# A table for the first nine tiles of a fused attention and MLP kernel, with earlier loads of two tiles and casts one tile further ahead

**The chip, the cores and the metric.** The kernel runs on one core of one Trainium2 chip. The metric is device time in microseconds (us), median of several executions; lower is better. An execution is called slow when it lies over 1.5% above the fastest of the same kernel. The ratios leave them out, the quoted medians and ranges do not; all profiles are of fast executions. The results are correct to the reference's tolerance unless a run is said to be wrong.

## The reference

A decayed linear attention (a state per head, multiplied by a factor per token) is followed by a dense layer with a SoLU activation, a layer norm and a second dense layer. Cut to what matters:

```python
B, H, S, D = 4, 8, 768, 64;  d_ff = 1024
for t in range(S):
    state = gamma * state + outer(k[:, :, t], v[:, :, t])
    y[:, :, t] = q[:, :, t] @ state / sqrt(D)
x = y, heads side by side            # [3072, 512]
h = x @ w_in                         # [3072, 1024]
u = h * softmax(h)
ln = (u - mean(u)) / sqrt(var(u) + 1e-6) * g_ln
out = ln @ w_out                     # [3072, 512]
```

The kernel works in chunks ("tiles") of 128 tokens: 4 batches of 6 tiles, 24 in all. Inside a tile the attention is matmuls; between tiles of a batch a state is carried on.

## The kernel before

One list of operations is written in Python. Each names its engine and what it reads and writes; the waits between engines are worked out from the list. So the place of an operation in the list sets its place in its engine's queue, and nothing else. For each tile `t`:

- loads of k, q, v by DMA; casts to bf16 (`ck`, `cq`, `cv`; the last also multiplies by the decay), mostly on Pool;
- transposes of k and q on TensorE into the PSUM bank `Tp`, evacuated to `qkT`;
- `scores` (TensorE into `PT`), `mask` (DVE), `inter` and `intra` (TensorE into `Yp`), `state` (TensorE into `Sp`) with its evacuation `st`, and `y` (DVE, makes `xT`);
- `mm1` (xT times w_in, into two halves of `Hp`), `expo` on ACT, `umul` on DVE (makes u), `square` on ACT and five tiny statistics on Pool;
- transposes of u into the same bank `Tp`, evacuated to `uT`; `mm2` (uT times the second weight, into `Zp`); `z_out`, which scales and stores.

The weights need work first: w_in is cast, w_out is multiplied by g (`w_g_cast`), its column mean is formed on TensorE, and `centre` subtracts it on DVE. Two first tiles use the uncentred weight and a correction, so that they need not wait for the centring.

The opening of the kernel before is written out by hand, and then a loop follows (cuts marked):

```python
loads(0)
load_w_in()
loads(1)
load_g()
load_w_out()
for t in range(2, NRAW):           # NRAW = 6
    loads(t)
setup_consts()
warm(5)                            # matmuls of zeros, they keep TensorE's clock up
cast_qk(0, "dve")
# ... cut: tile 0, tile 1, casts of the weights
for kt in range(KT2):
    colmean(kt)
colmean_out()
square(1)
cast_qk(2, "dve")
# ... cut
mm2(0)
z_out(0)                           # correction on DVE, then scaling on ACT, then the store
t_qk(2)                            # transposes, then qkT on ACT
for kt in range(3):
    centre(kt)
inter(2)
mm2(1)
scores(2)
mask(2)
z_out(1)
cast_qk(3)
cast_v(3)
t_qk(3)
for kt in range(3, 6):
    centre(kt)
intra(2)
state(2)
y_evac(2)
# ... cut: mm1 of tile 2 follows only here

for j in range(3, NT + 2):
    on(loads, j + 3)
    on(intra, j)
    on(state, j)
    on(scores, j + 1)
    on(casts, j + 2)
    # ... cut: t_qk(j+2), umul(j-1), y, st, square, stats, mask(j+1)
    on(mm2, j - 2)
    on(z_out, j - 2)
    # ... cut: t_u and u_evac of j-1, mm1 and expo of j, inter(j+1)
```

The softmax here doesn't subtract the row's maximum and nothing guards it: scores larger than these inputs give would overflow.

## Time and profile before

| | kernel before |
|---|---|
| time, median of the first 3 runs | 168.51 us (167.45 to 168.52) |
| span of the profiled run | 166.9 us |
| TensorE busy | 147.4 us, 88% |
| DVE, ACT, Pool busy | 72%, 64%, 57% |
| mean granted TensorE clock | 0.949 of full |
| mm1 of tile 2 starts at | 40.04 us |

The view gives, for each stretch of the span, the busy us of each engine with the number of instructions, the granted clock, the busy share of the 16 DMA engines and GB/s. Of the kernel before:

```profile
core 0: us, PE busy (x) PEld busy (x) DVE busy (x) ACT busy (x) POOL busy (x), PEclk, DMA share, GB/s
...
20.00:26.00 6.00, 5.13 (x17) 2.08 (x19) 4.87 (x11) 1.99 (x5) 4.38 (x6) 0.64 1.05 226
26.00:40.00 14.00, 8.46 (x76) 4.47 (x74) 10.62 (x16) 4.90 (x7) 10.59 (x15) 0.81 0.91 187
40.00:46.00 6.00, 5.74 (x46) 3.13 (x47) 5.10 (x10) 2.85 (x6) 0.52 (x2) 0.60 1.10 218
46.00:52.00 6.00, 4.93 (x62) 3.24 (x65) 4.15 (x8) 3.41 (x8) 3.79 (x8) 1.00 0.20 46
```

TensorE is busy for only 8.46 of 14 us in the second stretch, and in the first and third it is busy at little more than half speed. ACT is busy for 4.90 of 14: it mostly stands and waits. Note also the last line: DMA moves 46 GB/s there, although most of the tiles are still to be loaded.

### The profile page before, as it was taken

How to read it: one execution, taken by the hardware profiler on the slowest of the kernel's cores; microseconds unless marked ns; L12 is line 12 of the kernel's file. 1: busy time of each engine (PE TensorE's matmuls, PEld its weight loads, DVE VectorE, ACT ScalarE, POOL GpSimd, SP SyncE). 2: the span in 40 equal slices, each digit the busy share in tenths (PEclk: the TensorE clock that was granted, in tenths of full speed). 3: DMA queues.
4: the chain of work that ended last, by engine and by line, in shares of the span. 5: the costliest groups of instructions: out<-in, count | busy, mean ns of one | idle time of the engine just before them, and what ended most of it. 6: DMA issues, size and time to landing. Idle time of an engine off the chain costs nothing. (4 is left out here: it accounts for less than half of the span.)

```text
span 166.9 us, 3716 instructions
## 1 busy us (share of the span) xinstructions
PE 147.4 (88%) x1403; PEld 84.6 (51%) x1427; DVE 120.7 (72%) x231; ACT 106.4 (64%) x204; POOL 95.7 (57%) x197
## 2 busy tenths in 40 slices
PE   1995699565979999999999999999999999999962
PEld 0442434232546555666556555656565656555530
DVE  5275778859778767977787678877887789778540
ACT  7856334303657758776867587767775777667651
POOL 3201787980172885678557855696568656833430
PEclk9999559785699999999999999999999999999999
DMA  5999999976920877987899689896997699111102
GB/s 119 322 346 241 364 209 224 221 160 166 211 67 2 208 179 177 198 209 181 181 189 230 157 190 185 206 211 156 201 237 194 155 192 223 68 67 63 58 26 105
DMA packets 81058, 29.61 MB, mean 177 GB/s; under 512 B 76432, under 2 KB 76432, under 8 KB 81040
## 3 DMA queue, kind: packets, MB, share of 16 engines
q1 hardware_dynamic: 81040, 29.37, 75.2%
q8 instruction: 11, 0.18, 0.5%
q14 instruction: 7, 0.06, 0.1%
HBM read 23.07 MB, written 6.29 MB: 176 GB/s over the span
## 5 line engine op out<-in xcount | busy, mean ns | idle before, releaser
L412 PE MATMUL Hp<-w_in,xT 128*128 128x512 bf16 x188 | 47.9, 399 | 1.4 <-DVE xT L406 1.3
L471 PE MATMUL Zp<-w,uT 128*128 128x512 bf16 x157 | 37.5, 379 | 2.5 <-ACT out_sb L489 1.4
L339 ACT ACTIVATE qkT<-Tp 128x1024 bf16<-128x1024 bf16 x24 | 24.5, 1022 | 18.6 <-PE Tp L335 18.6
L354 DVE TENSOR_TENSOR ptm<-PT,tri 128x1024 bf16<-128x1024 f32 x24 | 29.2, 1216 | 6.5 <-PE PT L347 6.5
L412 PEld LDWEIGHTS Hp<-w_in,xT 128*128 128x128 bf16 x192 | 18.4, 101 | 20.2 <-issue 3.3
L471 PEld LDWEIGHTS Zp<-w,uT 128*128 128x128 bf16 x176 | 16.2, 98 | 17.5 <-DVE uT L465 1.5
L447 POOL TENSOR_SCALAR chain<-sq,chain 128x1 f32<-128x1 f32 x24 | 6.4, 266 | 30.8 <-ACT sq_junk L434 30.6
L419 ACT ACTIVATE e_1<-Hp 128x512 bf16<-128x512 f32 x24 | 14.3, 597 | 11.9 <-PE Hp L412 11.9
L419 ACT ACTIVATE e_0<-Hp 128x512 bf16<-128x512 f32 x24 | 14.3, 597 | 10.5 <-PE Hp L412 10.5
L465 DVE COPY uT<-Tp 128x1024 bf16<-128x1024 bf16 x24 | 16.4, 684 | 2.3 <-PE Tp L459 2.1
L406 DVE TENSOR_TENSOR xT<-Yp,ytab 128x512 bf16<-128x512 f32 x24 | 16.5, 686 | 0.2
L489 ACT ACTIVATE out_sb<-Zp,rstd 128x512 f32<-128x512 f32 x22 | 14.9, 679 | 2.1 <-PE Zp L471 2.1
L425 DVE CUSTOM_DVE_ANT_0 u_1<-Hp,e_1 128x512 bf16<-128x512 f32 x12 | 8.3, 691 | 9.3 <-ACT e_1 L419 9.3
L453 POOL TENSOR_TENSOR rstd<-chain,mhalf 128x1 f32<-128x1 f32 x24 | 13.2, 550 | 2.0
L425 DVE CUSTOM_DVE_ANT_0 u_0<-Hp,e_0 128x512 bf16<-128x512 f32 x12 | 8.3, 690 | 7.9 <-ACT e_0 L419 7.9
L434 ACT ACTIVATE sq_junk<-u_1 128x1024 bf16<-128x1024 bf16 x12 | 12.6, 1050 | 1.9 <-DVE su L425 1.9
L434 ACT ACTIVATE sq_junk<-u_0 128x1024 bf16<-128x1024 bf16 x12 | 12.6, 1050 | 0.9 <-DVE su L425 0.9
L441 POOL TENSOR_SCALAR chain<-se 128x1 f32<-128x1 f32 x24 | 6.5, 269 | 11.3 <-ACT e_0 L419 8.6
L425 DVE CUSTOM_DVE_ANT_0 u_1<-Hp,e_1,su 128x512 bf16<-128x512 f32 x12 | 9.0, 751 | 4.9 <-ACT e_1 L419 4.9
L347 PE MATMUL PT<-qkT 64*128 64x128 bf16 x192 | 9.8, 222 | 2.3 <-ACT qkT L339 2.2
L425 DVE CUSTOM_DVE_ANT_0 u_0<-Hp,e_0,su 128x512 bf16<-128x512 f32 x12 | 9.0, 751 | 3.6 <-ACT e_0 L419 3.6
L323 POOL TENSOR_TENSOR v_1<-v_raw,vtab 128x512 bf16<-128x512 f32 x6 | 6.3, 1043 | 8.4 <-DMA v_raw<-in_v_dram 8.3
(94 smaller groups left out, 251.8 us busy)
## 6 DMA issues: line engine op xcount, KB each, us to landing
k_raw<-in_k_dram SPq DMA_DIRECT2D x24, 256.0 KB, 3.7
q_raw<-in_q_dram SPq DMA_DIRECT2D x24, 256.0 KB, 4.3
v_raw<-in_v_dram SPq DMA_DIRECT2D x24, 256.0 KB, 4.6
out_dram<-out_sb SPq DMA_DIRECT2D x24, 256.0 KB, 2.2
w_in_st<-in_moe_w_in_dram SPq DMA_DIRECT2D x4, 512.0 KB, 5.7
w_out_st<-in_moe_w_out_dram SPq DMA_DIRECT2D x4, 512.0 KB, 5.3
g_sb<-in_moe_g_ln_dram SPq DMA_DIRECT2D x1, 4.0 KB, 4.4
```

The costliest lines, as they stand in the source:

```text
L339: op("act", lambda e: e.activation(out=qkT[sT][:], in_=Tp[:], func=ACT.Copy), w=[("qkT", sT)], ps=[("T", "r")])
L347: op("pe", lambda e, p=p, h2=h2, rows=rows: e.matmul(PT[:, 4 * h2 + p, :], qkT[sT][rows, 4 + p, :], qkT[sT][rows, p, :], start=True, stop= ...
L354: op("dve", lambda e: e.tensor_tensor(out=ptm[s][:], in0=PT[:], in1=tri[:].unsqueeze(1).to_broadcast([128, 8, 128]), op=ALU.mult), r=["tri ...
L406: op("dve", lambda e: e.tensor_tensor(out=xT[s][:], in0=Yp[:], in1=ytab[:, c, :, :], op=ALU.mult), r=[("ytab", p) for p in range(NPAIR)], ...
L412: op("pe", lambda e, kt=kt: e.matmul(Hp[:, hf, :], xT[s][:, kt, :], w_in16[:, kt, 512 * hf:512 * hf + 512], start=(kt == 0), stop=(kt == K ...
L419: op("act", lambda e: e.activation(out=e16[s][:, 512 * hf:512 * hf + 512], in_=Hp[:, hf, :], func=ACT.Exp, accum_out=se[ss][:, hf:hf + 1]) ...
L425: op("dve", lambda e: e.tensor_tensor_reduce(out=u16[s][:, 512 * hf:512 * hf + 512], in0=Hp[:, hf, :], in1=e16[s][:, 512 * hf:512 * hf + 512],
L434: op("act", lambda e: e.activation(out=sq_junk[:], in_=u16[s][:], func=ACT.Square, accum_out=sq[ss][:]), r=[("u16", s, 0), ("u16", s, 1)], ...
L453: op("pool", lambda e: e.tensor_tensor(out=rstd[ss][:], in0=ch[:, 3:4], in1=mhalf[:], op=ALU.pow), r=[("ch3", sc), "mhalf"], w=[("rstd", ss)])
L465: op("dve", lambda e: e.tensor_copy(out=uT[s][:], in_=Tp[:]), w=[("uT", s)], ps=[("T", "r")])
L471: op("pe", lambda e, kt=kt, w=w: e.matmul(Zp[:, :], uT[s][:, kt, :], w[:, kt, :], start=(kt == 0), stop=(kt == KT2 - 1)), r=[("uT", s), (w ...
L489: op("act", lambda e: e.activation(out=out_sb[so][:], in_=Zp[:], func=ACT.Copy, scale=rstd[ss][:, 0:1]), r=[("rstd", ss)], w=[("out_sb", s ...
```

## The change

Its intent is to keep TensorE fed from the start. The hand-written opening goes, and a table gives the order of all operations of the first nine tiles (and the regular part up to tile 12), and for some of them the engine. A local search made the table. Loads of tile 1 now come ahead of w_in and those of tile 2 (with k and q of tile 3) ahead of w_out; w_out's casts are on DVE and ACT, none on Pool any more; casts run up to three tiles ahead instead of two; there are eight raw buffers for each of q, k and v instead of six, and four sets of statistics instead of three. A store may stand apart from its output scaling. The core of the diff, cut:

```diff
+PROLOGUE = """
+Lk.0 ck.0 Lv.1 cv.1 Lq.0 cq.0:dve warm.6 clr.0 Lv.0 Lk.1 t_k.0 warm.6 t_q.0 qkT.0:dve warm.3 scores.0 cv.0
+state.0 Lq.1 Lwi.3 wi0.3:act mask.0 wi1.3:act ck.1 cq.1 Lwi.1 Lwi.2 wi1.1:act t_k.1 intra.0 wi0.1:act Lwi.0 st.0
+Lq.2 cq.2 t_q.1 Lk.2 qkT.1:dve wi1.2:act Lv.2 wi0.2:act Lq.3 y.0 ck.2 cv.2 state.1 Lk.3 Lwo.2 wi0.0:act warm.2
+scores.1 inter.1 mask.1 wi1.0:act Lg.0 Lwo.0 cq.3 warm.11 mm1_0.0 e0.0 Lwo.1 intra.1 mm1_1.0 ck.3 st.1:act Lwo.3
+Lv.3 y.1 u0.0 t_k.2 t_q.2 e1.0 qkT.2:dve Lk.4 u1.0 mm1_0.1 statsA.0 e0.1 state.2 inter.2 Lq.4 Lv.4 sq.0 stats.0
+scores.2 mm1_1.1 Lk.5 t_k.3 st.2 t_q.3 mask.2 u0.1 intra.2 y.2 Lq.5 Lv.5 Lk.6 qkT.3 warm.2 t_u0.0 Lq.6 e1.1
+inter.3 wg.4:dve Lv.6 wg.1:act wg.3:dve wg.5:dve Lk.7 t_u1.0 wg.6:dve wg.0:act scores.3 mask.3 wg.2:act wg.7:act
+mm1_0.2 warm.7 colmean.0 cv.3 state.3 intra.3 e0.2 u0.2 Lq.7 u1.1 Lv.7 Lk.8 Lq.8 Lv.8 Lk.9 uT.0:act Lq.9 Lv.9
+ck.4 cq.4 y.3 cm_out.0 ctr.4 ctr.1 t_k.4 ctr.5 ctr.7 mm1_1.2 ck.5 sq.1 t_q.4 qkT.4 e1.2 u1.2 mm2.0 st.3:act cq.5
... (some 20 more lines of the table are cut)
+"""
-    NRAW, N16, NQT, NOUT = 6, 4, 4, 4
+    NRAW, N16, NQT, NOUT = 8, 4, 4, 4
-        NST = 3
+        NST = 4
+        def evac(eng, out, in_, **deps):
+            if eng == "act":
+                op(eng, lambda e: e.activation(out=out, in_=in_, func=ACT.Copy), **deps)
+            else:
+                op(eng, lambda e: e.tensor_copy(out=out, in_=in_), **deps)
... (the stages take an engine now; their instructions are the same)
+        default = {"ck": "pool", "cq": "pool", "qkT": "act", "st": "dve", "uT": "dve", "z": "act"}
+        for item in PROLOGUE.split():
+            item, _, eng = item.partition(":")
+            name, t = item.rsplit(".", 1)
+            if name == "warm":
+                warm(int(t), None)
+            else:
+                put(name, int(t), eng or None)
+        for j in range(0, NT + 2):
+            for n in ("Lk", "Lq", "Lv"):
+                put(n, j + 5)
... (intra, state, scores, as before)
+            for n in ("ck", "cq", "t_k", "t_q", "qkT", "cv"):
+                put(n, j + 2)
+            for n in ("ck", "cq", "cv"):
+                put(n, j + 3)
... (the rest of the loop, as before; put() leaves out what the table has done)
```

In the table `L` is a load, `wi0.3` the cast of one half of w_in's slice 3, `wg` a cast of w_out, `ctr` a centring, `t_k` and `t_q` are input transposes, `t_u` transposes of u, `e` the exponential, `u` the product, `sq` the square, `clr` a matmul that clears the state. `:act` or `:dve` names the engine where it is not the default.

## The prediction

> **What bounds the kernel now.** I read first the page's 40 slices, then the time line of TensorE for the first matmul group (mm1, into Hp) of each tile, then single waits in the opening. In the slices a column is 4.17 us and a digit tenths.
>
> ```profile
> PE   1995699565979999999999999999999999999962
> PEclk9999559785699999999999999999999999999999
> DMA  5999999976920877987899689896997699111102
> ```
>
> TensorE is full from about the 12th slice; its holes lie before 50 us. So do all the slices with a low granted clock. DMA is full for the first eight slices and has a hole in slices 11 to 13. Next, mm1 of tiles 0, 1, 2, 4, 5, 6 and 23 on TensorE (start, duration):
>
> ```profile
> 12.12 1.67 PE L412 MATMUL Hp<-w_in,xT 128*128 128x512 bf16 x7
> ...
> 20.87 3.19 PE L412 MATMUL Hp<-w_in,xT 128*128 128x512 bf16 x7 [0.98 <-DVE xT L406]
> ...
> 40.04 3.59 PE L412 MATMUL Hp<-w_in,xT 128*128 128x512 bf16 x8 [0.31 <-DVE xT L406]
> ...
> 53.44 1.89 PE L412 MATMUL Hp<-w_in,xT 128*128 128x512 bf16 x8
> ...
> 58.79 1.89 PE L412 MATMUL Hp<-w_in,xT 128*128 128x512 bf16 x8
> ...
> 64.48 1.89 PE L412 MATMUL Hp<-w_in,xT 128*128 128x512 bf16 x8
> ...
> 156.59 1.67 PE L412 MATMUL Hp<-w_in,xT 128*128 128x512 bf16 x7
> ```
>
> From tile 4 to tile 23 the pitch is (156.59 - 53.44) / 19 = 5.43 us. The loop is TensorE's own work; the view by stretches gives TensorE 93.00 busy us of the 94 between 63 and 157. But the first four tiles took 53.44 us: 19 us between mm1 of tiles 1 and 2 alone. A steady pitch would have put tile 4 at 12.12 + 4 x 5.43 = 33.8. The opening is the loss. Two lines of TensorE's time line, and under them two of ACT's, show how it is lost:
>
> ```profile
> 35.22 0.62 PE L335 MATMUL Tp<-ident,qk_3 128*128 128x128 bf16 x8
> ...
> 39.12 0.61 PE L347 MATMUL PT<-qkT 64*128 64x128 bf16 x8 [1.97 <-ACT qkT L339]
> ```
>
> ```profile
> 37.43 0.72 ACT L485 ACTIVATE out_sb<-z_tmp,rstd 128x512 f32<-128x512 f32 x1 [6.33 <-DVE z_tmp L482]
> 38.06 1.01 ACT L339 ACTIVATE qkT<-Tp 128x1024 bf16<-128x1024 bf16 x1
> ```
>
> The transposes of tile 3 ended at 35.8. Their evacuation stood in ACT's queue behind an output that waited 6.33 us for DVE, which was busy centring w_out. TensorE idled 1.97 us, and its clock was lowered after such holes (granted 0.64 in 20 to 26 us, 0.60 in 40 to 46).
>
> **What the Trainium skill says.** (1) "TensorE: Matmul & The Clock Gate", Part 1, architectural detail: ACT and DVE are strict FIFO. The ACT lines above agree. That is why a mere reordering can pay. (2) The same page, "The HAM clock gate": an idle window of about 3.4 us halves the clock, a busy one restores it. The trace agrees in kind: eight mm1 matmuls take 3.59 us at 40.04 and 1.89 at 53.44. (3) "DMA: Bandwidth & Descriptors", Specifications: transfers under 512 B do not reach line rate. Agreed: q, k and v come in 256 B runs (76432 of 81058 packets are under 512 B), and one 256 KB load is consumed about every 1.15 us at the start (casts at 4.22, 5.38, 6.53), 228 GB/s. Two w_in slices of 512 KB came 1.4 us apart (casts at 10.50 and 11.90), 374 GB/s. (4) "GPSIMD Engine Reference", Specifications: Pool shares SBUF interfaces with VectorE. Agreed: a DVE cast that ran beside Pool took 1.268 us, its like alone 0.427.
>
> **The change, part by part.**
>
> *Loads.* The first loads become k0, v1, q0, v0, k1, q1, then w_in, then q2, k2, v2, q3, k3, then w_out. The first four tensors are not needed alone: mm1 of tile 0 now waits for 1.57 MB of tiles plus 2.1 MB of w_in instead of 0.79 + 2.1. At the spacings above: k0 at 4.2, then five loads at 1.15 give q1 at 10.0, then four slices at 1.3 to 1.4 give the last of w_in at about 15.3. ACT has two half casts left (about 0.6 each), so mm1 of tile 0 starts near 16.4: **4.3 us later** than now. In return tile 1 is ready with it. Before this, TensorE transposes and scores tiles 0 and 1, filled up with warming matmuls.
>
> *Work from 16.4 us to the end of mm1 of tile 4.* The table has, on TensorE, with the start-to-start pitches of 58 to 64 us: five mm1 at 1.73 (8.7), five input transposes at 0.67 (3.3), four scores at 0.33 (1.3), four inter at 0.32 (1.3), five intra at 0.30 (1.5), four state and a clear (1.3), three transposes of u at 0.45 (1.35), two mm2 at 1.52 (3.0), the column mean (8 x 0.22 = 1.7) and nine warming matmuls (1.9): **25.4 us**. DVE has: masks 3.4 at 1.14, y 4 x 0.60, u 4 x 1.50, two copies at 0.6, four w_out casts at 0.65, four centrings at 0.69 and one mean correction 0.8, about **19 us**. ACT, counted in the same way (eight exponentials 5.5, two squares 2.3, three qkT and three uT 5.7, four w_out casts 2.6, the rest 3), has **19 us**. The table moves st, uT and two output scalings between DVE and ACT to balance them. TensorE is the heaviest.
>
> *The waits in it.* I walked the table by hand through the five queues with these durations. TensorE is nearly always fed, since two tiles' fronts are ready before the first u. The places that wait: around 23.5 us for Tp (one bank serves qkT and uT), and 25 to 27 us for the last w_out slices, for which DVE's and ACT's casts stand in the queue ahead of mask(3) and e(2). There the table has seven warming matmuls. The walk ends mm1 of tile 4 at 43.4, that is 27.0 us for 25.4 of work. No walk of mine has all semaphore delays, slowed casts and clock dips, so I allow 1.6 us more: 45.0. Today it ends at 53.44 + 1.73 = 55.2.
>
> *What is then still owed.* At that point the new order has done one mm2 and one u transpose less (1.52 + 0.45), and inter, intra and a cleared state more (about 1.2): 0.8 us behind. Gain: 55.2 - 45.0 - 0.8 = **9.4 us**.
>
> *Afterwards.* Tiles 4 to 8 are TensorE-bound today already, so their order can only keep the gain; my walk of tiles 5 and 6 gave 5.4 us a tile. The loop after tile 12 is the old one, except that casts run three tiles ahead. TensorE waits there for no cast now, so that is worth nothing by itself. NRAW 8 and NST 4 only allow the table's reach. The tail (157 to 167, TensorE busy 5.33 of 10) is unchanged. 168.5 - 9.4 = 159.1; I say 159.5.
>
> **Rivals.**
>
> *A: loads bind the opening.* 16.4 depends on six 256 B-run loads at 1.15 us. In 26 to 40 us DMA moved only 187 GB/s, 1.4 us a load. Loads as slow as that would put the first mm1 at 17.7 and, by w_out, the column mean 2 to 3 us later. For it: DMA is full in the first eight slices. Against: the casts at 4.22 to 6.53 show the faster rate just there. It would make 162 to 164.
>
> *B: in-order queues jam.* A table tuned to modelled durations can place an operation ahead of one that is ready, as z did above, at 25 to 27 us most likely, or uT and squares on ACT from 39 to 46 us, where ACT's list is dense. Stores stand in SP's queue behind loads up to tile 11, so store(0) could leave late and hold the fourth output buffer; I expect it out around 48 us and needed around 57. Each hole also risks half clock for a window of 3.4 us (1.7 us). Two such: 162 to 163.
>
> *C: the walk is right and the clock never falls.* 157 to 158.
>
> *D: nothing gained,* if the later start (4.3 us) and 14 more warming matmuls (37 against 23) eat it. By 55.2 us today's order has done about 28 us of TensorE work, counted with the same pitches (five mm1, three mm2, the column mean, seven input transposes, six scores, four u transposes, the rest 4.3), so 27 are lost. The new order has about 3.3 us of useful work behind it at 16.4, so 13 lost; no view shows what would eat the other 14. Unlikely.
>
> **Range and chances.** C bounds it below at about 156.5; A or B alone gives up to 163.5. Slower than 165.2 (2%) would need A and B together and more. Faster 0.93, same 0.05, slower 0.02.
>
> **What would show it.** mm1 of tile 0 near 16.4 (right for loads, 17.7 for rival A); mm1 of tile 1 within 5 us of it; mm1 of tile 2 between 24 and 27 instead of 40.04; mm1 of tile 4 ending at 43 to 47; mm1 pitch afterwards still 5.43; the PEclk row without 5s after the fifth slice; TensorE busy us about unchanged or lower with a shorter span. I am wrong if the loop's pitch changes (casts one tile further ahead would then matter, or a store holding z), or if a single wait of more than 3 us appears on TensorE between 16 and 45 us.

## The result, and the profile after

| | before | after |
|---|---|---|
| time, median of 4 runs each | 167.98 us (167.18 to 168.52) | 161.38 us (161.09 to 161.62) |
| span of the profiled run | 166.9 us | 159.9 us |
| TensorE busy | 147.4 us | 146.6 us |
| DVE / ACT busy | 120.7 / 106.4 us | 113.9 / 110.9 us |
| mean granted clock | 0.949 | 1.000 |

The ratio is 0.961, with a 95% interval from 0.9557 to 0.9663. (Ratios are the mean time of one kernel's fast runs over that of the other's of the same rounds, so they are not quite the ratios of the medians quoted.) The change is faster by 3.9%, 6.6 us by the medians, 7.0 us by the two profiled spans.

The slices of the page, 4.0 us each, after:

```profile
PE   1979979689997999999999999999999999999961
PEclk9999999999999999999999999999999999999999
DMA  5999989999989999998991099999888310111112
```

The holes in TensorE's row are gone but for a few tenths, the clock row has no 5 any more, and DMA stays full until about 84 us, where it pauses, instead of pausing at 46 to 54. Then mm1 on TensorE. In the opening the table issues its two halves apart, four matmuls each. The lines are, in order, the first half of tile 0, the second of tile 1, the first and second of tile 2, the second of tile 4, the first of tile 5, and the whole of tiles 6, 10 and 23:

```profile
16.30 1.04 PE L451 MATMUL Hp<-w_in,xT 128*128 128x512 bf16 x4
...
21.97 1.04 PE L451 MATMUL Hp<-w_in,xT 128*128 128x512 bf16 x4
...
25.68 1.04 PE L451 MATMUL Hp<-w_in,xT 128*128 128x512 bf16 x4
...
32.61 1.03 PE L451 MATMUL Hp<-w_in,xT 128*128 128x512 bf16 x4
...
44.90 1.04 PE L451 MATMUL Hp<-w_in,xT 128*128 128x512 bf16 x4
...
49.93 1.03 PE L451 MATMUL Hp<-w_in,xT 128*128 128x512 bf16 x4
...
55.50 1.89 PE L451 MATMUL Hp<-w_in,xT 128*128 128x512 bf16 x8
...
79.33 1.89 PE L451 MATMUL Hp<-w_in,xT 128*128 128x512 bf16 x8
...
149.33 1.89 PE L451 MATMUL Hp<-w_in,xT 128*128 128x512 bf16 x8
```

Tile 0 starts 4.2 us later than before, and tile 2's first half 14.4 us earlier. Tile 4's mm1 ends at 45.8 (its successor starts 0.87 us after its second half's start) against 55.2. By tile 10, where both kernels have come to the same order, the gain is 86.38 - 79.33 = 7.05 us, and it stays: from tile 10 to tile 23 the pitch is (149.33 - 79.33) / 13 = 5.38 us, before it was (156.59 - 86.38) / 13 = 5.40. (The line of the kernel before at 156.59 has seven matmuls of eight; with the missing record about 0.2 us earlier, the two pitches are the same.) From tile 6 to tile 10 the new kernel takes longer, 23.8 us against 21.9: there it makes up an mm2 and a u transpose that it had put off. TensorE's busy time hardly moved. What went is idle time and time at half clock before 55 us.

What still waits after the change? TensorE's two longest idle stretches between 12 and 100 us:

```profile
31.58 0.32 PE L435 MATMUL Sp<-v_3,qk_3 128*64 128x64 bf16 x8 [1.18 <-POOL v_3 L361]
...
49.70 0.40 PE L375 MATMUL Tp<-ident,qk_3 128*128 128x128 bf16 x4 [0.93 <-POOL qk_3 L349]
```

Behind both stands Pool (buffer 3 is tile 3 in the first, tile 7 in the second). Pool's time line:

```profile
30.48 1.04 POOL L361 TENSOR_TENSOR v_3<-v_raw,vtab 128x512 bf16<-128x512 f32 x1 [6.09 <-DMA v_raw<-in_v_dram]
...
47.47 0.61 POOL L349 CAST qk_3<-k_raw 128x512 bf16<-128x512 f32 x1
48.05 1.04 POOL L361 TENSOR_TENSOR v_3<-v_raw,vtab 128x512 bf16<-128x512 f32 x1
49.03 0.61 POOL L349 CAST qk_3<-q_raw 128x512 bf16<-128x512 f32 x1
```

The first waited 6.09 us for its load. The others waited for nothing: Pool was simply behind with its own list. And DVE, in the stretch where it might have worked ahead, stood for a load of w_out:

```profile
27.77 0.88 DVE L312 TENSOR_SCALAR w_g<-w_out_st,g_sb 128x512 bf16<-128x512 f32 x2 [2.84 <-DMA w_out_st<-in_moe_w_out_dram]
```

### The profile page after: what moved, and what is told of

Its sections match the earlier page's. It is cut to its first block, busy times and chain, and to the rows that moved or that the text cites. A ratio compares the mean times of both kernels' runs of the same rounds, so it can differ in the third digit from the quotient of the medians.

```text
span 159.9 us, 3767 instructions
## 1 busy us (share of the span) xinstructions
PE 146.6 (92%) x1441; PEld 82.3 (51%) x1441; DVE 113.9 (71%) x222; ACT 110.9 (69%) x215; POOL 94.9 (59%) x198
## 5 line engine op out<-in xcount | busy, mean ns | idle before, releaser
L451 PE MATMUL Hp<-w_in,xT 128*128 128x512 bf16 x192 | 46.8, 380 | 0.0
L513 PE MATMUL Zp<-w,uT 128*128 128x512 bf16 x176 | 41.6, 379 | 1.4 <-ACT out_sb L310 1.4
L368 ACT ACTIVATE qkT<-Tp 128x1024 bf16<-128x1024 bf16 x19 | 19.4, 1023 | 14.8 <-PE Tp L375 14.7
L451 PEld LDWEIGHTS Hp<-w_in,xT 128*128 128x128 bf16 x192 | 17.1, 98 | 16.6 <-ACT w_in L310 0.5
L310 ACT ACTIVATE out_sb<-Zp,rstd 128x512 f32<-128x512 f32 x19 | 12.9, 679 | 3.5 <-PE Zp L513 2.8
L370 DVE COPY uT<-Tp 128x1024 bf16<-128x1024 bf16 x17 | 11.7, 686 | 4.0 <-PE Tp L502 3.9
L340 PE MATMUL Zp<-ones_bf,zeros_bf 128*128 128x512 bf16 x37 | 10.8, 431 | 3.5 <-DVE zeros_bf L299 3.5
L480 POOL TENSOR_SCALAR chain<-se 128x1 f32<-128x1 f32 x24 | 7.0, 292 | 6.8 <-ACT e_0 L458 4.5
L483 POOL TENSOR_SCALAR chain<-su 128x1 f32<-128x1 f32 x24 | 6.9, 288 | 5.3 <-DVE su L464 3.9
```

The lines of the kernel that those rows point to most:

```text
L310: op(eng, lambda e: e.activation(out=out, in_=in_, func=ACT.Copy, scale=scale), **deps)
L340: op("pe", lambda e: e.matmul(Zp[:], zeros_bf[:], ones_bf[:].unsqueeze(1).to_broadcast([128, 4, 128]), start=True, stop=True), r=["zeros_b ...
L368: op(eng, lambda e: e.activation(out=out, in_=in_, func=ACT.Copy), **deps)
L370: op(eng, lambda e: e.tensor_copy(out=out, in_=in_), **deps)
L451: op("pe", lambda e, kt=kt: e.matmul(Hp[:, hf, :], xT[s][:, kt, :], w_in16[:, kt, 512 * hf:512 * hf + 512], start=(kt == 0), stop=(kt == K ...
L513: op("pe", lambda e, kt=kt, w=w: e.matmul(Zp[:, :], uT[s][:, kt, :], w[:, kt, :], start=(kt == 0), stop=(kt == KT2 - 1)), r=[("uT", s), (w ...
```

## The experiments

My theory was that the order of the computing in the opening makes the gain, that it needs the early loads of tiles 1 and 2, and that late loads and in-order queues are what keeps it from being larger. Rivals tested: the load order alone; one jam alone (an output that waits on ACT ahead of a qkT evacuation); the warming matmuls; the choice of engines; the earlier casts. The comparison goes by the ratio. The runs came in three, the first on another chip than the other two: the first four, the next four, the last four. Three parts of the change have no run of their own: the eight raw buffers, the four sets of statistics, and w_out's casts taken off Pool. Of the first the trace says something: between 40 and 157 us TensorE of the kernel before waits for no cast or load (its longest wait there is 0.96 us, for a uT), so in its loop as it stands there was nothing for more buffers to gain. Of the third: a w_out cast took 1.57 us on Pool (at 17.43), 0.72 on ACT (at 17.36); what that is worth is open.

### The load order, from both sides

**a_old_loads.** The table's computing with the loads of the kernel before.

```diff
-Lk.0 ck.0 Lv.1 cv.1 Lq.0 cq.0:dve ...
+Lk.0 Lq.0 Lv.0 Lwi.0 Lwi.1 Lwi.2 Lwi.3 Lk.1 Lq.1 Lv.1 Lg.0 Lwo.0 Lwo.1 Lwo.2 Lwo.3 (tiles 2 to 5: Lk, Lq, Lv) ck.0 cv.1 cq.0:dve ...
```

> New kernel, its table kept for all computing, but the first 26 loads in the order of the kernel before (tile 0, w_in, tile 1, g, w_out, tiles 2 to 5). My theory (the gain is the order of the computing, and it needs tiles 1 and 2 early): k, q and v of tile 2 then land at about 22 to 26 us instead of 16.8 to 19.9, mm1 of tile 0 still waits in TensorE's order for tile 1, and the time is about 165 us (163.5 to 166.5), more than half of the gain lost. Rival that load order is all of the gain: 168. Rival that load order does not matter: 161.4.

Measured: 166.70 us (166.22 to 167.64), ratio to before 0.992 (0.9849 to 0.9991). The list of TensorE's waits shows the cause in its first line (waiting line, what it waited for, us in total, times, longest):

```profile
PE Sp L434 <- POOL v L360: 7.5, 1, 7.5
```

In the table v of tile 1 is Pool's second cast, so all that follows on Pool stands until it lands; mm1 of tile 0 starts at 24.61. Some 5 of the 6.6 us are lost. This one wait accounts for all of it: once mm1 has begun, tile 4's second half follows 25.1 us later (49.69), against 28.6 in the new kernel. The table and its load order belong together. That no table made for the old loads could do as well is not shown; none was tried.

**b_new_loads.** The reverse: the kernel before with tiles 0 and 1, w_in, tile 2, g, w_out, then the rest.

```diff
 loads(0)
-load_w_in()
 loads(1)
+load_w_in()
+loads(2)
 load_g()
 load_w_out()
-for t in range(2, NRAW):
+for t in range(3, NRAW):
```

> Kernel before, only its loads reordered: tiles 0 and 1, w_in, tile 2, g, w_out, then 3 to 5. My theory: mm1 of tile 0 moves from 12.1 to about 16 us, that of tile 1 stays near 20, tile 2 still near 40, because the order of computing holds it: 167.5 to 169. Rival that early tiles are the gain: 162 to 164.

Measured: 171.29 us (170.37 to 172.11), ratio 1.0184 (1.0104 to 1.0264), slower by more than I thought (whether by 2% is not clear, the interval holds it). mm1 of tiles 0, 1 and 2 begins at 13.96, 23.93 and 42.11 us, against 12.12, 20.87 and 40.04. Early tiles are no use to an order that does not use them, and they push the weights back. The rival that early loads alone are the gain is refuted.

### The warming matmuls

**a_few_warm.** The last 25 of the 37 warming matmuls are dropped.

```diff
-... t_q.0 qkT.0:dve warm.3 scores.0 ... warm.2 ... warm.11 ... warm.2 ... warm.7 ...
+... t_q.0 qkT.0:dve scores.0 ...
```

> New kernel without the last 25 of its 37 warming matmuls (the first twelve stay). My theory: they fill waits, so no time is won by dropping them, and the granted clock falls in at least one window of the first 35 us: 162.5 to 164. Rival that they are mere filler: 161.4 within 0.5. Rival that they cost TensorE time: 159.5 to 160.5.

Measured: 160.57 us (160.24 to 160.84), ratio 0.9548 (0.9486 to 0.9609). My expectation failed: it is not slower. The clock did fall; of this kernel the clock row and mm1 of tile 0:

```profile
PEclk9999579999999999999999999999999999999999
```

```profile
15.93 1.89 PE L450 MATMUL Hp<-w_in,xT 128*128 128x512 bf16 x4 [1.65 <-ACT w_in L309]
```

The bracket gives the idle time before it and what ended it, here the last cast of w_in. Four matmuls took 1.89 us instead of 1.04, and mm1 of tile 1's second half started at 23.27 instead of 21.97. But by then TensorE was ahead of the loads anyway; the column mean, which waits for w_out, began at 27.85 instead of 28.07. Whether the kernel is even a little faster without them is not settled: the 0.8 us come from different calls, and the intervals of the two ratios overlap. In this profile the second w_out piece was used 1.1 us earlier (26.61 against 27.77), for no reason that I can name: its load was issued earlier, and w_out's first load was issued at 17.28, where it was issued at 18.42 to 18.77 in the profiles of the new kernel, the control, a_casts_two, a_short_table and a_mended.

### The choice of engines

**a_default_engines.** The table's order is kept, but its engine suffixes on qkT, st, uT and z, and on one q cast, are dropped.

```diff
-... qkT.1:dve ... st.1:act ... uT.0:act ... st.3:act ... uT.1:act ... z.3:dve ...
+... qkT.1 ... st.1 ... uT.0 ... st.3 ... uT.1 ... z.3 ...
```

> New kernel with the table's choices of engine for the evacuations of qkT, st and uT, for z and for one cast undone (qkT and z on ACT, st and uT on DVE, cast of q on Pool; the first cast of q stays on DVE). My theory: DVE gets some 10 copies of 0.6 us more than it gives, it was busy 7.39 of 8 us between 32 and 40, so the opening gets 1 to 2 us longer: 162.4 to 163.5. Rival that the order alone does it: 161.4 within 0.5.

Measured: 167.80 us (166.43 to 169.59), ratio 0.9978 (0.9856 to 1.0101). Most of the gain is gone, several times what I had expected. How much is less sure than the ratio looks: two executions took 166.4 and 166.7 us, one 168.9, and the slow one 169.6. The profile is of the fastest. There TensorE first waits 1.91 us (at 14.57) for tile 1's qkT, which on ACT stands behind casts of w_in; that is made up by tile 2, whose first half starts at 25.91 against 25.68. Then an mm2 that took 1.89 us in the new kernel took 3.30 at a lowered clock (0.62 in 34 to 38 us), and the next new wait of over a microsecond follows:

```profile
34.24 3.30 PE L511 MATMUL Zp<-w_g,uT 128*128 128x512 bf16 x8
...
46.51 0.62 PE L373 MATMUL Tp<-ident,qk 128*128 128x128 bf16 x8 [1.72 <-DVE uT L368]
```

And what DVE did before it let that copy through:

```profile
43.98 1.21 DVE L398 TENSOR_TENSOR ptm<-PT,tri 128x1024 bf16<-128x1024 f32 x1
45.11 0.74 DVE L331 SCALAR_TENSOR_TENSOR w<-w_out_st,g_sb,m_sb 128x512 bf16<-128x512 f32 x1
45.77 0.68 DVE L368 COPY uT<-Tp 128x1024 bf16<-128x1024 bf16 x1
```

The transposes of u had ended at 43.07 (started 42.45, 0.62 us), but the bank `Tp` came free only at 46.45, after a state copy, a mask and a centring in DVE's queue. All transposes of inputs need the same bank. With the copy on ACT (40.83 in the new kernel, right after the transposes) this wait does not exist. Tile 4's mm1 is 4.2 us later than in the new kernel (second half at 49.06 against 44.90), tile 10's first half 4.8 us, after a wait of 1.69 us (at 74.78) for an output scaling that was put back on ACT.

The queue is one way to read this, the sum of DVE's work another, and the edit does not part them. In the stretch that matters DVE has no room. The new kernel, then this run (columns as before):

```profile
30.00:46.00 16.00, 14.14 (x157) 7.94 (x158) 15.30 (x27) 14.12 (x26) 11.61 (x16) 1.00 1.10 215
...
30.00:50.00 20.00, 15.70 (x151) 8.28 (x149) 18.63 (x34) 10.21 (x21) 13.87 (x22) 0.91 1.10 213
```

DVE is busy for 15.30 of 16 us already in the new kernel; the five copies of uT and st that come back to it here, at 0.6 us each, are 3 us more, while ACT falls to 10.21 of 20.

### How much of the table is needed

**a_short_table.** The table is cut after its last centring; the loop does the rest.

```diff
-... ctr.2 ctr.0 statsA.1 mm1_0.4 state.6 mm1_1.4 (and 20 more lines)
+... ctr.2 ctr.0
```

> New kernel with its table cut after the last centring of w_out (about 45 us into it); what follows is emitted by the kernel's ordinary loop. My theory: the gain is made by then and the rest of the table only has to keep it, so the time is 161.4 within 1 us. Rival that the table's order of tiles 5 to 12 matters: 163 or more.

Measured: 163.81 us (162.52 to 164.07), ratio 0.9708 (0.9642 to 0.9773). I expected less loss; TensorE waits 2.4 us once (up to 46.05), in Zp for DVE's correction of a first output, and the eight matmuls after it took 3.53 us instead of 1.89, at a lowered clock. So the ordinary order is not good enough until the two first outputs are away, and the part of the table after them is worth some 2 us.

### Are loads the bound?

**a_long_runs** and **b_long_runs** read q, k and v of tiles 0 to 5 in rows of 2 KB (eight tokens of one head) in place of eight runs of 256 B. Bytes, buffers and waits are unchanged. Their outputs are wrong, which doesn't matter for the times.

```diff
+if t < 6:
+    flat = src.rearrange("b h (s x) d -> (b h s) (x d)", x=8)[128 * t:128 * t + 128, :]
+    op("sp", lambda e: e.dma_start(out=dst[:].rearrange("p h d -> p (h d)"), in_=flat), ...)
+    return
```

> New kernel, wrong result on purpose: q, k and v of tiles 0 to 5 are read as rows of 2 KB instead of eight runs of 256 B, with the same bytes and waits. If loads bind the opening, as I think: the last w_in lands 2 to 3 us earlier, v of tile 3 too, and the time falls by 2 to 4 us to 157.5 to 159.5. Rival that the order and the in-order queues bind it: 161 or more.

> Kernel before with the same long runs for tiles 0 to 5, wrong on purpose. My theory: its opening is bound by the order of DVE and ACT work from 20 us on, not by loads, so it wins under 1.5 us: 166.5 to 168. Rival that loads bind both kernels alike: a fall of 2 to 4 us as in the new kernel, 164 to 166.

Measured, new kernel: 158.52 us (158.42 to 158.99), ratio 0.9415 (0.9365 to 0.9464), as my theory had it: some 2.9 us less than the 161.38 of the real loads (or the 161.39 of the control below, on the same chip). Kernel before: 166.26 us (165.22 to 166.75), ratio 0.9878 (0.9815 to 0.9941), that is 1.2%, 2.1 us by the ratio's 0.9878 of 168.7; a little more than I had allowed. So loads cost both openings something; the new one more by these figures, but the difference of 0.8 us is within the intervals. In the new one even this gain is capped. Its time line on TensorE:

```profile
13.90 2.54 PE L345 MATMUL Zp<-ones_bf,zeros_bf 128*128 128x512 bf16 x11
16.27 1.03 PE L456 MATMUL Hp<-w_in,xT 128*128 128x512 bf16 x4
```

ACT had ended its last w_in cast at 14.25, but mm1 stood behind the eleven warming matmuls that the table had put there for slower loads, and began at the same 16.3 as before. What did move is v of tile 3, cast at 23.86 instead of 30.48.

### The hand-made alternative

**b_hand_order.** In the kernel before, tile 2's and tile 3's fronts go ahead of the two first outputs, and all centring goes behind mm1 of tile 2.

```diff
+t_qk(2); inter(2); scores(2); mask(2)
 mm2(0)
-z_out(0); t_qk(2); centre(0..2); inter(2); mm2(1); scores(2); mask(2); z_out(1)
 cast_qk(3); cast_v(3); t_qk(3)
-centre(3..5)
 intra(2); state(2); y_evac(2); st_evac(2); casts(4); scores(3)
-mask(3); mm1(2), expo(2); centre(6..7); t_qk(4)
+z_out(0); mm1(2), expo(2); mask(3); mm2(1); z_out(1); t_qk(4)
 # in the loop at j == 3
+    centre(0..3) after mask(4), centre(4..7) after u_evac(2)
```

> Kernel before with a small reorder by hand and nothing else: tile 2's front and tile 3's before the two first outputs, mm2 of tile 1 and all centring after mm1 of tile 2, so that no qkT evacuation stands behind an output that waits for DVE. My theory: mm1 of tile 2 starts near 32 to 34 instead of 40.04, some of it is given back when centring lands on tiles 3 and 4: 164 to 166. Rival that the jam of outputs and centring is all of the difference: 161 to 162.5. Rival that it is worth nothing: 168.

Measured: 169.07 us (167.83 to 169.89), ratio 1.0029 (0.9948 to 1.0109): nothing. mm1 of tile 2 did start at 34.64 instead of 40.04. But TensorE's time line has a new wait, and DVE's time line tells why:

```profile
46.81 1.03 PE L335 MATMUL Tp<-ident,qk 128*128 128x128 bf16 x8 [4.22 <-DVE uT L465]
```

```profile
42.71 3.45 DVE L301 SCALAR_TENSOR_TENSOR w<-w_out_st,g_sb,m_sb 128x512 bf16<-128x512 f32 x4
46.08 0.68 DVE L465 COPY uT<-Tp 128x1024 bf16<-128x1024 bf16 x1
```

The centring that I had moved away from one tile stood in front of the evacuation of another, and the wait came back at a third place. mm1 of tile 4 began at 54.53, after the 53.44 of the kernel before.

**b_hand_act.** The same with uT of tiles 0 to 3 and st of tiles 1 to 3 evacuated on ACT.

```diff
-op("dve", lambda e: e.tensor_copy(out=uT[s][:], in_=Tp[:]), ...)
+op("act" if t < 4, activation(..., func=ACT.Copy), ...)      # and st the same for 1 <= t < 4
```

> The hand-reordered kernel before, with the evacuations of uT for tiles 0 to 3 and of st for tiles 1 to 3 put on ACT; no other edit. If what the hand order lacked is the choice of engine (its TensorE waited 4.22 us for a uT copy that stood on DVE behind four centrings), mm1 of tile 4 starts near 49 to 51 us instead of 54.53 and the time is 164 to 166. Rival that it lacked early loads: 168 or more, because the opening then waits for q, k and v.

Measured: 167.57 us (167.10 to 168.61), ratio 0.9936 (0.9874 to 0.9999). The wait of 4.22 us is gone, and 0.62 is left of it. But uT of tile 1 now stood on ACT behind a square (TensorE waited 2.28 us for it), the column mean waited 0.85 and 1.09 us for casts of w_out on Pool, and tile 5's transposes 1.22 and 0.62 for other Pool casts. mm1 of tile 4 began at 53.09. Neither number that I had written came true: two of the table's ideas by hand are worth half a per cent. What separates this from the new kernel is a list of waits, not one cause.

### The casts one tile further ahead, and a mended table

**after_again.** The new kernel unchanged, as a control for the rest.

> The new kernel unchanged, as the control for the other three runs on the same chip: 161.4 within 0.5, ratio to the kernel before 0.961.

Measured: 161.39 us (161.03 to 161.95), ratio 0.9576 (0.953 to 0.9622).

**a_casts_two.** The loop casts two tiles ahead again.

```diff
-            for n in ("ck", "cq", "cv"):
-                put(n, j + 3)
```

> New kernel without the line in its loop that casts three tiles ahead, so that tiles 17 to 23 are cast two ahead again. My theory: TensorE waits for no cast in the loop, so the same as the control within 0.3 us. Rival that the earlier casts are part of the gain: 0.5 us or more slower.

Measured: 161.42 us (161.18 to 161.82), ratio 0.9585 (0.9545 to 0.9624). It is the same as the control. In the loop the earlier casts are worth nothing, and TensorE never waited for a cast there. The table's own early casts are not tested by this.

**a_mended.** The table with some entries moved. The second product u of tile 1, the mask of tile 3 and mm1 of tile 2 go ahead of w_out's casts; tile 1's u is transposed ahead of tile 4's k; nine warming matmuls go; and on Pool tile 7's casts of k and q go ahead of the statistics of tiles 2 and 3.

```diff
-e1.1 inter.3 wg.4:dve wg.1:act wg.3:dve wg.5:dve t_u1.0 wg.6:dve wg.0:act scores.3 mask.3 wg.2:act wg.7:act mm1_0.2 warm.7 colmean.0
+e1.1 inter.3 u1.1 wg.4:dve wg.1:act t_u1.0 scores.3 mask.3 mm1_0.2 mm1_1.2 e0.2 wg.0:act wg.2:act wg.3:dve wg.5:dve e1.2 u0.2 wg.6:dve wg.7:act uT.0:act colmean.0
... (Pool, order of its list)
-statsA.1 statsA.2 stats.1 statsA.3 ck.7 cv.7 cq.7 stats.3 stats.2
+statsA.1 stats.1 ck.7 cq.7 statsA.2 statsA.3 cv.7 stats.2 stats.3
```

> New kernel with its table mended for loads that land later than it supposes: u of tile 1's second half, the mask of tile 3 and the second half of mm1 of tile 2 are put ahead of the w_out casts that wait for their load (DVE idled 2.84 us there), tile 1's u is transposed before tile 4's k, nine warming matmuls of that stretch are dropped, and on Pool the casts of tile 7 go ahead of the statistics of tiles 2 and 3. My theory (in-order queues behind late loads, and one late cast, cost about 2 us): 159 to 160. Rival that the loads alone bind until 48 us: no better than 161.

Measured: 160.13 us (159.85 to 160.35), ratio 0.9503 (0.9465 to 0.954), all six runs below all six of the control, 1.3 us faster. Where it comes from can be read off the start of mm1 of tiles 4 and 5 (first halves). In the mended kernel:

```profile
43.24 1.04 PE L450 MATMUL Hp<-w_in,xT 128*128 128x512 bf16 x4
...
48.39 1.03 PE L450 MATMUL Hp<-w_in,xT 128*128 128x512 bf16 x4
```

In the profiles of the new kernel they start at 43.68 and 49.93, and in the control at 44.29 and 50.27. So the stretch before tile 4, which I had reordered most, won only 0.4 to 1.1 us. Pool's casts of tile 5's k and q still waited 1.78 us each for their loads there, but TensorE waited for neither; its own longest wait in that stretch is 1.12 us (at 36.05), for tile 4's qkT. That loads bind there is shown by a_long_runs, not by this run. The other 0.8 to 1.1 us come with tile 7's transposes, which no longer wait for Pool (0.93 and 0.67 us in those two profiles). What the nine dropped warming matmuls contribute is not separated. This version beats both kernels.

## Why the prediction was right, point by point

The time lay inside the range (156.5 to 163.5), and the direction and the place were right. The gain was too large: 9.0 us was said, 6.6 came (7.0 by the spans). It lay in the part of the range that was left for rivals A and B. Something of both came, but later than they were placed: see below.

- **First mm1 at 16.4: right.** It was 16.30. The loads of the first 16 us came as reckoned (q of tile 1 cast at 10.16, the last of w_in at 15.62). Faster loads would not have made it earlier: in a_long_runs eleven warming matmuls held it at 16.27.
- **mm1 of tile 2 between 24 and 27: half right.** The first half began at 25.68, the second at 32.61.
- **mm1 of tile 4 ending at 45.0: 0.8 us too early** (45.8). The sum of TensorE's work held: added up from start to start on the time line, I estimate 25.3 of the 29.5 us as work and 4.2 as waits, where the prediction had 25.4 and 3.2 (1.6 of the walk, 1.6 of allowance). Two of its terms were misread and nearly cancel: mm2's pitch is 1.73, not 1.52, and a pair of input transposes takes 0.45 to 0.54, not 0.67 (a matmul record is missing between them in the lines of 58 to 64 us). The allowance for waits was 1 us too small. The term that was off is the loads after 16 us, which I kept at the opening's rate: DMA moved 204 and 188 GB/s in the slices of 16 to 24 us, v of tile 3 was cast at 30.48, and DVE's and ACT's last casts of w_out began at 29.23, where the walk had them at 25 to 27. (The last three w_out pieces came 1.4 us apart, at 26.40, 27.77 and 29.23, as reckoned.) That is of rival A's kind, later than A had it. a_long_runs shows that loads bind in the opening; it does not give the size of this term, since it makes all loads of tiles 0 to 5 faster than the prediction had them. Why these loads were slow is open.
- **"My walk of tiles 5 and 6 gave 5.4 us a tile": failed.** From the end of tile 4's mm1 to the end of tile 6's, at 57.3, it took 11.5 us instead of 10.8. The trace shows one wait of 0.93 us in it, for a Pool cast of tile 7. This is rival B, on an engine that I had not named. a_mended removed it.
- **The rest.** The prediction missed 9.4 - 7.0 = 2.4 us of span: 0.8 by tile 4, 0.93 on Pool, and some 0.6 between tiles 4 and 10 that no wait shows. It is work, not waiting: from 57.30 to 79.33 TensorE is busy for all of the 22.03 us. Some 0.2 of it is the mm2 owed at tile 4, at 1.73 instead of 1.52; the rest stays open.
- **"The table moves st, uT and two output scalings between DVE and ACT to balance them": right, and badly undervalued.** The prediction gave it no size and called reordering the reason why the change can pay. a_default_engines shows that the same order without these choices keeps little of the gain. The prediction's sums of busy time hid this, because they were too small and taken over too long a stretch: it had 19 us of DVE work in 28, with four of the eight centrings. The trace has all eight before 45.3 us, and 23.06 us of DVE work in the 29.64 from 16.30 to 45.94 (ACT 22.55), of which 15.30 in the 16 us from 30 to 46. Where DVE is that full there is no room for the copies that are put back on it, and TensorE waits for the PSUM banks that they empty.
- **The clock: right as a description; as a cause it depends on the place.** The clock row is full after the change, but a_few_warm has half clock for two slices and is not slower: up to there TensorE has slack until w_out is there. Where it has none the half clock counts, as rival B said. In a_default_engines the slow product at 34.24 is followed by an mm1 that is 1.37 us late (38.24 against 36.87), the one before it being 0.27 late; in a_short_table the matmuls at 46.05 took 1.64 us more. The holes ahead of it need not be long: in the 4 us before 34 TensorE was busy for 2.15, and its longest wait was 1.17.
- **"Worth nothing by itself" on the casts: right for the loop** (a_casts_two).
- **Rival D: wrong, as said.** The 14 additional warming matmuls cost nothing that I can measure with certainty.
- **Small slips in its readings.** DMA's hole is in slices 12 and 13, not 11 to 13, and it is full for slices 2 to 8. The line at 156.59 lacks a record, so the pitch is nearer 5.42 than 5.43. None matters to the sum.

## What to carry to other kernels

When one engine is full in the loop and starved in the opening, count first what has to be loaded by when, then sum each engine's work over the fullest stretch and not over the whole opening, and then ask for each shared PSUM bank which queue its evacuation stands in, and behind what. A reordering by hand that removes the longest wait can leave the time unchanged, because the moved work stands in front of the next evacuation; order and choice of engine have to be found together. A table found by search is tuned to the load times and durations that it supposed: its own fillers and its order on a lightly loaded engine are the first places to look when the real ones differ.

## What the Trainium skill lacked or had wrong

- "TensorE: Matmul & The Clock Gate", Terms, gives the penalty of a throttled clock as the throttled time times one minus the ratio. As a cost of the kernel it is only an upper bound, since it leaves out slack: without 25 warming matmuls, TensorE ran at a granted 0.5 and 0.7 for two slices of 4 us, and the kernel took 160.57 us against 161.38 (it also had those matmuls less to do). In a_default_engines, without slack, one mm2 of 3.30 us instead of 1.89 put the next mm1 1.1 us further behind.
- The same page's Part 1 says that the default state is throttled. The durations here agree (the first six warming matmuls took 2.74 us, 0.46 each, later eleven took 2.54), but the profile's granted clock shows full speed in those first microseconds. The page warns in general that clock events in a trace can be unreliable, not that they are missing before the first change.
- "DMA: Bandwidth & Descriptors", Specifications, names 512 B as the least size for line rate, and the page has no measured rate for loads in shorter runs on this chip (only a reckoned overhead for 256 B). Here 256 B runs gave 1.15 us for 256 KB in the opening (228 GB/s), and 2 KB rows for six tiles shortened the new kernel by 2.9 us.
